# One Strassen level for the output projection of a gated mixer: w_out after wo, on row-scaled float16 y

## The chip, the cores and the metric

The kernel runs on one core of a Trainium2 chip. Its engines are TensorE (PE; its weight loads are listed as PEld), VectorE (DVE), ScalarE (ACT), GpSimd (POOL) and SyncE (SP), which issues all the transfers here. Each engine works through its own queue in program order; engines meet at semaphores. The metric is the device time of one execution in microseconds (us); of each kernel several executions were timed, and one more was profiled.

## The reference

With x of 2048 x 1024, the kernel computes

```python
g = sigmoid((x * gate_w).sum(-1, keepdims=True))
# a: 32 heads of 32; query s looks at keys s, s-2, ..., s-14
a = sliding_attention(x @ wqkv) @ wo            # wo: 1024 x 1024
z = gelu(x @ w_in)                              # w_in: 1024 x 3584
z1, z2 = z[:, :1792], layernorm(z[:, 1792:])
y = z1 * (w_sp @ z2 + b_sp[:, None])            # w_sp: 2048 x 2048
out = g * a + (1 - g) * (y @ w_out)             # w_out: 1792 x 1024
```

## The kernel before

All large buffers are slices of one SBUF tile, `arena`, so the profile names nearly every operand "arena"; line numbers tell them apart. A product is a run of matmuls over 128-row slices of the inner dimension that accumulate in one PSUM bank (`ps`, eight banks); an engine then copies the bank out.

TensorE's work comes in this order: two z2 column blocks of the first two row tiles and three more tiles of the first block (L577 to L579); heads of group 0 (`qkv_tile`, L535) and of groups 1 to 7, with the rest of z2's first block after group 1 (L580); the other z2 columns (L605); z1 (L624 to L642); the w_sp product (`g_group`, L669, called for n = 0 to 15; matmuls on L650); the w_out product (L728 to L736, matmuls on L734, 14 per bank, 32 banks); the wo product (L746 to L757, matmuls on L751, 8 per bank, 32 banks). VectorE computes attention, in steps of up to 4.4 us, from the first heads until far into the w_sp product, and DVE work of the other stages is put between those steps.

The order on the engines is written by a planner, `Beat` (L207). It counts TensorE's columns (`run`) as its clock. `at(t, fn)` puts `fn` on a heap, and at the end of each product (`run`, then `flush`) all that has come due is issued at that place of the program. Attention steps are issued by the planner when its count of VectorE's backlog falls under 3 us. So a due time fixes a place in each engine's queue, not a time: whatever stands there waits for its inputs, and all behind it on that engine waits too.

The w_sp product is already one Strassen level. Group n handles rows 256u to 256u+255 (u = n // 2) and half `fb` = n % 2 of the columns, with seven products of eight 448-column matmuls on float16 operands. Their sums t1 to t4 of z2 (`t_sums`, L463, and L643; the operation is on L461) and s1 to s4 of w_sp rows (`s_sums`, L454) are made on VectorE. In Python's words:

```python
product(pa, v.a11, b11, fb, True)     # P1
p1 = keep(pa, lo)                     # ScalarE copies the bank
product(pb, v.a12, b21, fb, True)     # P2
vec(g[:, 0, 0], pb[:, 0:ZC], p1)      # VectorE
product(pa, v.s2, t2, fb, False)      # P3 accumulates on P1's bank
u2 = keep(pa, lo)
product(pd, v.s1, t1, fb, True)       # P4
p5 = keep(pd, None)
product(pa, v.s3, t3, fb, False)      # P5
```

P6 accumulates in `pd` on P4, and P7 in `pa` on P5; after P7 ScalarE writes the last quarter (L689), and VectorE multiplies the whole by z1 (L690, `z` is the ring slot that held z1). `store_y` writes y to DRAM, from where it comes back transposed (`load_yT`, L507) as the stationary side of the w_out product. w_sp rows are scaled by a power of two per row (`row_norm`, L421; `row_power`, L424), so that float16 holds them; `omr` undoes it in the copy of w_out's banks (L735), and L740 adds the wo product times g.

SP's queue holds in order what the planner issues: w_sp rows by transposing DMA (`load_rows`, L443), z1 (`load_z1`, L492), y stores, transposed y, transposed attention outputs (`load_oT`, L415), w_out in two column halves (`load_w_out`, L510), wo (`load_wo`, L412).

## Time and profile before

| | us |
|---|---|
| median of 3 runs (698.88 to 702.46) | 699.11 |
| profiled execution | 699.66 |
| its span, first to last instruction | 697.9 |
| TensorE busy | 687.8 |
| VectorE busy | 467.8 |
| ScalarE busy | 293.5 |
| w_sp product, from its first matmul to w_out's | 370.4 to 542.4 |
| last attention step on VectorE | 484.6 |
| end of the last matmul | 694.1 |

A profile line such as "532.67 1.09 DVE L690 TENSOR_TENSOR arena<-arena 128x1792 bf16<-128x1792 bf16 x1 [1.55 <-ACT arena L689]" gives start and length in us, engine, line of the kernel, operation, output and inputs with their shapes, how many instructions were merged, and in brackets how long the engine stood idle before and what released it. SPq lines are the issuing of transfers, not the transfers. Rows of groups give busy time and the mean of one in ns. The chain of work that ended last is followed backwards from the last instruction through what released each step.

### The profile page before, as it was taken

Reading aid. Unit: us, or ns where it says so; the run is one execution under the profiler, and the core shown is the slowest. Engines: PE = TensorE matmul, PEld = TensorE weight load, DVE = VectorE, ACT = ScalarE, POOL = GpSimd, SP = SyncE. Lnnn points to the kernel's source line nnn. Section 1 sums busy time; section 2 is a strip of 40 time slices with the busy share of each in tenths; the row PEclk is TensorE's granted clock in tenths of the full one; section 3 lists DMA queues with packets and bytes.
Section 4 is the critical chain, followed back from the end, with each engine's and each line's share of the span. In section 5 each row is a group of like instructions: output and inputs, shape, how many; then the busy total and the mean of one; then the engine's idle time right before and its main releaser. Section 6 shows DMA issues by size and latency. Waiting matters only on the chain.

```text
span 697.9 us, 9291 instructions
## 1 busy us (share of the span) xinstructions
PE 687.8 (99%) x3667; PEld 401.0 (57%) x3681; DVE 467.8 (67%) x446; ACT 293.5 (42%) x562; POOL 13.7 (2%) x23
## 2 busy tenths in 40 slices
PE   8999999999999999999998999999999999999998
PEld 4577788888875555555554555555555444444443
DVE  0009899999999999999999999797552100001443
ACT  4255756565546968758332232322232222221000
POOL 1000000000000001021100000000000000000000
PEclk9999999999999999999999999999999999999999
DMA  8999649989869464534437655767999999000222
GB/s 238 180 244 259 189 105 269 258 240 235 220 169 246 173 212 139 165 113 165 149 103 212 115 146 144 200 166 174 179 213 256 214 199 234 1 0 16 75 76 76
DMA packets 234188, 118.13 MB, mean 169 GB/s; under 512 B 191009, under 2 KB 223521, under 8 KB 234145
## 3 DMA queue, kind: packets, MB, share of 16 engines
q1 hardware_dynamic: 234144, 117.54, 64.8%
q8 instruction: 29, 0.48, 0.3%
q14 instruction: 15, 0.11, 0.1%
HBM read 58.20 MB, written 37.82 MB: 138 GB/s over the span
## 4 chain that ended last, share of the span: by engine, by line
PE 95%; SPq 2%; DMA 1%; issue 1%; ACT 0%; DVE 0%; DVEq 0%
PE ps L535 24%; PE ps L650 23%; PE ps L634 14%; PE psb L734 14%; PE ps L281 12%; PE psa L751 8%; SPq L520 1%; DMA arena<-in_A_wqkv_dram 1%; DMA arena<-z_d 1%; SPq L518 0%; DVE arena L461 0%; SPq L249 0%; ACT L322 0%; SPq L516 0%; ACT arena L689 0%
## 5 line engine op out<-in xcount | busy, mean ns | idle before, releaser
L650 PE MATMUL ps<-arena 128*128 128x448 f16 x896 | 170.0, 353 | 2.2 <-DVE arena L461 2.0
L535 PE MATMUL ps<-arena 128*128 128x384 bf16 x1024 | 168.2, 328 | 2.4 <-DMA arena<-in_A_wqkv_dram 2.4
L535 PEld LDWEIGHTS <-arena 128*128 128x128 bf16 x1024 | 142.2, 139 | 28.5 <-issue 4.3
L650 PEld LDWEIGHTS <-arena 128*128 128x128 f16 x896 | 87.5, 98 | 84.6 <-DVE arena L461 2.5
L740 DVE SCALAR_TENSOR_TENSOR arena<-psa,g_s,arena 128x512 bf16<-128x512 f32 (+2 forms) x33 | 24.2, 735 | 126.5 <-PE psa L751 125.6
L304 DVE TENSOR_TENSOR arena<-arena 128x8192 bf16<-128x8192 bf16 x16 | 70.8, 4423 | 45.2 <-DMA arena<-k_d 44.9
L281 PE MATMUL ps<-arena 128*128 128x448 bf16 (+1 forms) x512 | 97.5, 353 | 0.1
L634 PE MATMUL ps<-arena 128*128 128x448 bf16 x512 | 97.2, 353 | 0.0
L734 PE MATMUL psb<-arena 128*128 128x512 bf16 x439 | 96.4, 379 | 0.5
L307 DVE TENSOR_TENSOR arena<-arena 128x4096 bf16<-128x4096 bf16 (+1 forms) x64 | 77.5, 1211 | 1.8
L634 PEld LDWEIGHTS <-arena 128*128 128x128 bf16 x512 | 49.9, 98 | 46.7
L281 PEld LDWEIGHTS <-arena 128*128 128x128 bf16 x512 | 49.9, 98 | 46.7 <-ACT arena L268 0.2
L734 PEld LDWEIGHTS <-arena 128*128 128x128 bf16 x448 | 43.8, 98 | 52.9
L543 ACT CAST arena<-ps 128x384 bf16<-128x384 f32 x112 | 51.1, 483 | 54.3 <-PE ps L535 51.8
L337 DVE TENSOR_TENSOR arena<-arena,att_A 128x8192 bf16<-128x8192 bf16 x16 | 70.8, 4422 | 0.7 <-DMA arena<-v_d 0.4
L662 ACT ACTIVATE arena<-ps,bt 128x448 f32<-128x448 f32 x48 | 30.4, 633 | 68.4 <-PE ps L650 68.4
L751 PE MATMUL psa<-arena 128*128 128x512 bf16 (+2 forms) x259 | 55.2, 373 | 0.3
L735 ACT ACTIVATE arena<-psb,omr 128x512 f32<-128x512 f32 x32 | 22.0, 687 | 74.8 <-PE psb L734 72.4
L636 ACT ACTIVATE arena<-ps 128x448 bf16<-128x448 f32 x64 | 33.5, 546 | 41.4 <-PE ps L634 34.7
L287 ACT ACTIVATE arena<-ps 128x448 bf16<-128x448 f32 x64 | 34.6, 549 | 25.3 <-PE ps L281 24.9
L751 PEld LDWEIGHTS <-arena 128*128 128x128 bf16 x264 | 25.5, 98 | 30.1
L343 DVE TENSOR_TENSOR arena<-arena 128x4096 bf16<-128x4096 bf16 x16 | 36.6, 2288 | 0.3
(77 smaller groups left out, 365.4 us busy)
## 6 DMA issues: line engine op xcount, KB each, us to landing
arena<-in_B_w_sp_dram SPq DMA_DIRECT2D x16, 512.0 KB, 4.4
arena<-k_d SPq DMA_DIRECT2D x8, 960.0 KB, 7.1
arena<-v_d SPq DMA_DIRECT2D x8, 960.0 KB, 5.2
z_d<-arena SPq DMA_DIRECT2D x16, 448.0 KB, 4.8
arena<-z_d SPq DMA_DIRECT2D x16, 448.0 KB, 3.7
y_d<-arena SPq DMA_DIRECT2D x32, 224.0 KB, 2.9
arena<-in_A_wqkv_dram SPq DMA_DIRECT2D x24, 256.0 KB, 6.6
arena<-in_B_w_in_dram SPq DMA_DIRECT2D x6, 896.0 KB, 6.6
```

The source lines that it names most:

```text
L281: nc.tensor.matmul(ps[:, 0:N], xT[:, kt, i * P:(i + 1) * P], w2[:, kt, ZC * c:ZC * c + N], start=(kt == 0), stop=(kt == KT - 1))
L287: nc.scalar.activation(z2[:, i, ZC * c:ZC * (c + 1)], ps[:, 0:ZC], ACT.Gelu_apprx_tanh, accum_out=s1[:, 4 * i + c:4 * i + c + 1])
L304: TT(prod.rearrange("p (w j c) -> p w j c", w=W, j=8, c=C), in0, in1, ALU.mult)
L307: return lambda: TT(pv[:, :, 0:half], pv[:, :, 0:half], pv[:, :, half:2 * half], ALU.add)
L337: TT(prod.rearrange("p (w j d h) -> p w j d h", w=W, j=8, d=DH, h=HG), in0, in1, ALU.mult)
L343: return [(4.4, mul), (2.3, lambda: TT(p3[:, 0:4, :], p3[:, 0:4, :], p3[:, 4:8, :], ALU.add)), (1.2, lambda: TT(p3[:, 0:2, :], p3[:, 0:2, ...
L535: nc.tensor.matmul(ps[:, 0:3 * C].rearrange("p (t c) -> p t c", t=3), lhsT, wgt[:, 0:3, kt, :], start=(kt == 0), stop=(kt == KT - 1))
L543: nc.scalar.copy(st[:, j % 4, :], ps[:, 0:3 * C])
L634: nc.tensor.matmul(ps[:, 0:ZC], xT[:, kt, i * P:(i + 1) * P], w1[:, kt, :], start=(kt == 0), stop=(kt == KT - 1))
L650: nc.tensor.matmul(ps[:, 0:ZC], w[:, k, :], v[:, k, fb * ZC:(fb + 1) * ZC], start=(first and k == 0), stop=(k == 7), skip_group_check=True)
L734: nc.tensor.matmul(psb[:], yT[a % 11][:, f, :], w_out_sb[c][:, f, :], start=(f == 0), stop=(f == NF - 1))
L751: nc.tensor.matmul(psa[:, 0:c1 - c0], oT[a][:, kt, :], wo_sb[:, kt, c0:c1], start=(kt == 0), stop=(kt == KT - 1))
```

## The change

- The wo product comes directly after the w_sp groups. Its banks are copied by ScalarE into `mix`, times g. wo and the transposed attention outputs are loaded as soon as attention has ended, beside the w_sp groups.
- The w_out product comes last and is one Strassen level: for each 256 rows, seven products of seven 512-column matmuls, on float16.
- For float16, y is scaled by a power of two per row. After each group, ScalarE sums |y| (`y_norm`, two instructions); after each second group VectorE makes the powers (`y_power`), ScalarE scales y in place (`y_scale`, four instructions), and SP stores it and loads the z1 of two pairs later (`y_done`). The multiply's ring of z1 slots is filled four ahead at the start.
- Beside the wo product, w_out is loaded in two halves, VectorE finds its largest magnitude (`w_peak`), a matmul with ones spreads it over the partitions (`w_power`), ScalarE and VectorE scale it in place (`w_scale`), and VectorE makes the sums (`w_sums`, `y_sums`).
- Six z2 tiles instead of three stand ahead of the first heads.
- t4 is made with the other sums, which come due 62 instead of 71 us after the start of the z1 stage; the last w1 block moves to another place in the arena and is loaded later.
- Buffers move: rows of y, w_out, its sums, wo and the output slots take over areas of the earlier stages.

```diff
--- before.py
+++ after.py
...
-    y_d = dpool.tile([S, FH], BF, name="y_d")
+    y_d = dpool.tile([S, FH], F16, name="y_d")
...
-                for o in (T4_OFF, T4_OFF + 3584, T2_OFF, T4_OFF)]
+                for o in (T4_OFF, T4_OFF + 3584, T2_OFF, SN_OFF)]
...
+    w_out_n = reg(X_OFF, NF * D)
+    w_out_h = reg(X_OFF, NF * D).bitcast(F16)
+    wv = w_out_h.rearrange("p (h k n) -> p h k n", h=2, n=D)
+    d11, d12, d21, d22 = [wv[:, h, :, 512 * c:512 * (c + 1)] for h in range(2) for c in range(2)]
+    e1, e2, e4 = [reg(F_OFF + 3584 * r, 3584).bitcast(F16).rearrange("p (k n) -> p k n", n=512) for r in range(3)]
+    e3 = d12
...
+    class Rows:
+        def __init__(self, off):
+            y = [reg(off + 1792 * r, 1792).bitcast(F16).rearrange("p (k t) -> p k t", t=P) for r in range(2)]
+            self.whole = y
+            self.a11, self.a12, self.a21, self.a22 = [y[r][:, 7 * h:7 * h + 7] for r in range(2) for h in range(2)]
+            self.s1, self.s2, self.s3 = [reg(off + 3584 + 896 * r, 896).bitcast(F16).rearrange(
+                "p (k t) -> p k t", t=P) for r in range(3)]
+            self.s4 = self.a21
...
+          for o in [A_OFF + 1024 * r for r in range(11)] + [S0_OFF + 1024 * r for r in range(5)]]
+    wo_sb = reg(A_OFF + 11264, KT * D).rearrange("p (k n) -> p k n", k=KT)
...
-        beat.at(t + 1.0, lambda: store_o(NG - 1))
+        beat.at(t + 1.0, attended)
+
+    def attended():
+        store_o(NG - 1)
+        load_wo()
         prep["attended"] = True
-        beat.at(max(t, prep["mixed"]) + 2.0, load_all_oT)
-
-    def load_all_oT():
-        for n in range(16):
-            beat.at(beat.now + 3.5 * n, lambda n=n: load_oT(n))
-
-    prep = {"at": 1e12, "normed": 0, "done": False, "mixed": 0.0, "attended": False, "y": 0}
...
-    def load_oT(n):
-        sync.dma_start_transpose(oT[n], o_d[n * P:(n + 1) * P, :])
+    def load_oT(limit):
+        n = prep["o"]
+        if n < limit:
+            sync.dma_start_transpose(oT[n], o_d[n * P:(n + 1) * P, :])
+            prep["o"] += 1
...
     def t_sums():
-        return [column_sum(o, a, b, fb) for o, a, b in ((t1, b12, b11), (t3, b22, b12), (t2, b22, t1))
+        return [column_sum(o, a, b, fb) for o, a, b in ((t1, b12, b11), (t3, b22, b12), (t2, b22, t1), (t4, b21, t2))
                 for fb in range(2)]
...
+    def load_rows_y(u):
+        for r in range(2):
+            sync.dma_start_transpose(rows[u % 5].whole[r], y_d[(2 * u + r) * P:(2 * u + r + 1) * P, :])
+
+    def y_norm(n):
+        for r in range(2):
+            k = 2 * (2 * (n // 2) + r) + n % 2
+            nc.scalar.activation(g_slots[n % 2][:, r], z1_ring[n % 4][:, r], ACT.Abs, accum_out=yl[:, k:k + 1])
+
+    def y_power(u):
+        sl = slice(2 * u, 2 * u + 2)
+        pair = yl[:, 4 * u:4 * u + 4].rearrange("p (r b) -> p r b", b=2)
+        TT(ys[:, sl], pair[:, :, 0], pair[:, :, 1], ALU.add)
+        nc.vector.tensor_scalar(ys[:, sl], ys[:, sl], 2.0 ** -30, 2.0 ** -11, ALU.max, ALU.mult)
+        nc.vector.tensor_scalar(ys[:, sl].bitcast(U32), ys[:, sl].bitcast(U32), EXPO, EXPO,
+                                ALU.bitwise_and, ALU.bitwise_xor)
+        beat.on_vector(0.3)
+
+    def y_scale(u):
+        for n in (2 * u, 2 * u + 1):
+            for r in range(2):
+                nc.scalar.activation(y_ring[n % 4][:, r], z1_ring[n % 4][:, r], ACT.Copy,
+                                     scale=ys[:, 2 * u + r:2 * u + r + 1])
+
+    def y_done(u):
+        store_y(2 * u)
+        store_y(2 * u + 1)
+        if u + 2 < NU:
+            load_z1(2 * u + 4)
+            load_z1(2 * u + 5)
...
-    for i in range(2, 5):
+    for i in range(2, 8):
         z2_tile(i, 0)
...
-            for i in range(5, 16):
+            for i in range(8, 16):
                 z2_tile(i, 0)
...
     t = beat.now
-    prep["at"] = t + 71.0
-    prep["mixed"] = t + (16 * 4 * KT + 2 * NU * 56) * ZC * BEAT
+    prep["at"] = t + 62.0
...
             load_w1(2)
-        if c == 1:
-            load_w1(3)
         for i in range(16):
+            if c == 2 and i == 6:
+                load_w1(3)
...
-    for fb in range(2):
-        column_sum(t4, b21, t2, fb)()
-        beat.on_vector(2.0)
...
+    def product(ps, w, v, c0, c1, first):
+        K = v.shape[1]
+        for k in range(K):
+            nc.tensor.matmul(ps[:, 0:c1 - c0], w[:, k, :], v[:, k, c0:c1], start=(first and k == 0),
+                             stop=(k == K - 1), skip_group_check=True)
+        beat.run(K * (c1 - c0))
...
         TT(z, g, z, ALU.mult)
         beat.on_vector(1.1)

-    for n in range(3):
+    for n in range(4):
         load_z1(n)
     for n in range(2 * NU):
         u, fb = n // 2, n % 2
         t = beat.now
...
+        if fb == 0 and u + 1 < NU:
+            beat.at(t + 0.5, lambda u=u: load_scale(u + 1))
+            for h in range(2):
+                beat.at(t + 0.5, lambda u=u, h=h: load_rows(u + 1, h))
         g_group(n)
-        if n + 3 < 2 * NU:
-            load_z1(n + 3)
-        beat.at(beat.now + 2.0, lambda n=n: store_y(n))
+        y_norm(n)
+        if fb == 1:
+            beat.at(beat.now + 2.0, lambda u=u: y_power(u))
+            beat.at(beat.now + 6.0, lambda u=u: y_scale(u))
+            beat.at(beat.now + 9.0, lambda u=u: y_done(u))
+        elif u + 1 < NU:
+            for h in range(2):
+                scale_rows(u + 1, h)
+            beat.on_vector(2.5)
+            for fn in s_sums(u + 1):
+                fn()
+            beat.on_vector(2.8)
         if prep["attended"]:
-            for m in range(2):
-                beat.at(beat.now + 3.0, lambda u=u: load_yT(min(2 * u, 11)))
-        if u + 1 < NU:
-            if fb == 0:
-                for h in range(2):
-                    scale_rows(u + 1, h)
-                beat.on_vector(2.5)
-                for fn in s_sums(u + 1):
-                    fn()
-                beat.on_vector(2.8)
+            limit = 16 if n >= 2 * NU - 3 else 11
+            for m in range(6):
+                beat.at(beat.now + 1.0 + 1.6 * m, lambda limit=limit: load_oT(limit))
+    assert prep["attended"]
...
     t = beat.now
-    assert prep["attended"]
-    beat.at(t + 0.5, lambda: load_w_out(1))
-    for m in range(11):
-        beat.at(t + 2.6, lambda: load_yT(11))
-    beat.at(t + 40.0, load_wo)
...
-    work = [(a, 0) for a in range(4)] + [(a, 1) for a in range(4)] + [(a, c) for a in range(4, 16) for c in range(2)]
-    for a, c in work:
-        if 0 < a < 6 and c == 1:
-            beat.at(beat.now + 0.5, lambda: load_yT(16))
-        psb = psum.tile([P, 512], F32, name="psb", tag="ps")
-        for f in range(NF):
-            nc.tensor.matmul(psb[:], yT[a % 11][:, f, :], w_out_sb[c][:, f, :], start=(f == 0), stop=(f == NF - 1))
-        nc.scalar.activation(mix[a][:, 512 * c:512 * (c + 1)], psb[:], ACT.Copy, scale=omr[:, a:a + 1])
-        beat.run(NF * 512)
-    beat.flush(1e9)
...
+    for m in range(16):
+        beat.at(t + 1.0 + 1.6 * m, lambda: load_oT(16))
+
+    def load_w_out(h):
+        sync.dma_start(w_out_n[:, 7168 * h:7168 * (h + 1)].rearrange("p (k n) -> p k n", n=D),
+                       B_w_out.rearrange("(h k p) n -> h p k n", h=2, p=P)[h])
...
+    ones = zeros[:].rearrange("p g c -> p (g c)")
...
+    def w_peak(h):
+        w = [w_out_n[:, 7168 * h + 896 * m:7168 * h + 896 * (m + 1)] for m in range(8)]
+        top, low = abs_waste[:, 0:896], abs_waste[:, 896:1792]
+        for out_, op in ((top, ALU.max), (low, ALU.min)):
+            TT(out_, w[0], w[1], op)
+            for m in range(2, 8):
+                TT(out_, out_, w[m], op)
+        nc.vector.scalar_tensor_tensor(top, low, -1.0, top, ALU.mult, ALU.max)
+        nc.vector.tensor_reduce(wl[:, h:h + 1], top, AX.X, ALU.max)
+
+    def w_power():
+        TT(wl_n[:], wl[:, 0:1], wl[:, 1:2], ALU.max)
+        ps = psum.tile([P, 512], F32, name="ps", tag="ps")
+        nc.tensor.matmul(ps[:, 0:1], ones, wl_n[:], start=True, stop=True)
+        nc.vector.tensor_scalar(wsc[:], ps[:, 0:1], 2.0 ** -30, 2.0 ** -11, ALU.max, ALU.mult)
+        nc.vector.tensor_scalar(wsc[:].bitcast(U32), wsc[:].bitcast(U32), EXPO, EXPO, ALU.bitwise_and, ALU.bitwise_xor)
+
+    def w_scale(m):
+        sl = slice(2048 * m, 2048 * (m + 1))
+        if m < 3:
+            nc.scalar.activation(w_out_h[:, sl], w_out_n[:, sl], ACT.Copy, scale=wsc[:])
+        else:
+            nc.vector.tensor_scalar(w_out_h[:, sl], w_out_n[:, sl], wsc[:], None, ALU.mult)
+
+    def omegas():
+        for x in (ys[:], wsc[:]):
+            nc.vector.tensor_scalar(x.bitcast(U32), x.bitcast(U32), EXPO, EXPO, ALU.bitwise_and, ALU.bitwise_xor)
+        nc.vector.scalar_tensor_tensor(omr[:], ys[:], 0.5, omr[:], ALU.mult, ALU.mult)
+        nc.vector.tensor_scalar(omr[:], omr[:], wsc[:], 0.5, ALU.mult, ALU.mult)
+
+    def w_sums():
+        for out_, a, b in ((e1, d12, d11), (e2, d22, e1), (e3, d22, d12), (e4, d21, e2)):
+            TT(out_, a, b, ALU.subtract)
+
+    def y_sums(u):
+        v = rows[u % 5]
+        TT(v.s1, v.a21, v.a22, ALU.add)
+        TT(v.s3, v.a11, v.a21, ALU.subtract)
+        TT(v.s2, v.s1, v.a11, ALU.subtract)
+        TT(v.s4, v.a12, v.s2, ALU.subtract)
+
+    beat.at(t + 0.5, lambda: load_w_out(0))
+    beat.at(t + 9.5, lambda: load_w_out(1))
+    beat.at(t + 1.0, lambda: nc.vector.memset(zeros[:], 1.0))
+    beat.at(t + 11.0, lambda: w_peak(0))
+    beat.at(t + 19.0, lambda: w_peak(1))
+    beat.at(t + 31.0, w_power)
+    for m in range(7):
+        beat.at(t + 31.5 + 2.0 * (m % 3), lambda m=m: w_scale(m))
+    beat.at(t + 37.0, w_sums)
+    beat.at(t + 39.0, omegas)
+    for u in range(2):
+        beat.at(t + 26.0 + 4.0 * u, lambda u=u: load_rows_y(u))
+        beat.at(t + 44.0 + 4.0 * u, lambda u=u: y_sums(u))

     for a in range(16):
-        cuts = [0, 512, D] if a < 15 else [0, 512, 896, D]
-        for c0, c1 in zip(cuts, cuts[1:]):
+        if a == 12:
+            beat.at(beat.now + 0.5, lambda: load_rows_y(2))
+        for c in range(2):
             psa = psum.tile([P, 512], F32, name="psa", tag="ps")
             for kt in range(KT):
-                nc.tensor.matmul(psa[:, 0:c1 - c0], oT[a][:, kt, :], wo_sb[:, kt, c0:c1],
+                nc.tensor.matmul(psa[:], oT[a][:, kt, :], wo_sb[:, kt, 512 * c:512 * (c + 1)],
                                  start=(kt == 0), stop=(kt == KT - 1))
-            combine(psa, a, c0, c1)
-            if a == 15:
-                store(a, c0, c1)
-        if a < 15:
-            store(a, 0, D)
+            nc.scalar.activation(mix[a][:, 512 * c:512 * (c + 1)], psa[:], ACT.Copy, scale=g_s[:, a:a + 1])
+            beat.run(KT * 512)
+    beat.flush(1e9)
...
+    def hold(ps, scale):
+        out = keeps[kept[0] % 7]
+        kept[0] += 1
+        nc.scalar.activation(out, ps[:], ACT.Copy, scale=scale)
+        return out
...
+    def finish(out, ps, scale, x):
+        nc.vector.scalar_tensor_tensor(out, ps[:], scale, x, ALU.mult, ALU.add)
+
+    for u in range(NU):
+        v = rows[u % 5]
+        lo, hi = [omr[:, 2 * u + h:2 * u + h + 1] for h in range(2)]
...
+        pa, pb, pd = [psum.tile([P, 512], F32, name="ps", tag="ps") for _ in range(3)]
+        if u == 0:
+            for n in (3, 4):
+                load_rows_y(n)
+        product(pa, v.a11, d11, 0, 512, True)
+        p1 = hold(pa, lo)
+        product(pb, v.a12, d21, 0, 512, True)
+        TT(p1, p1, m11, ALU.add)
+        finish(o11, pb, lo, p1)
+        product(pa, v.s2, e2, 0, 512, False)
+        u2 = hold(pa, lo)
+        product(pd, v.s1, e1, 0, 512, True)
+        p5 = hold(pd, hi)
+        TT(u2, u2, m12, ALU.add)
+        product(pa, v.s3, e3, 0, 512, False)
+        u3 = hold(pa, hi)
+        TT(p5, p5, m22, ALU.add)
+        if 0 < u < NU - 1:
+            y_sums(u + 1)
+        product(pd, v.s4, d22, 0, 512, False)
+        TT(o22, p5, u3, ALU.add)
+        finish(o12, pd, lo, u2)
+        sync.dma_start(out2[2 * u * P:(2 * u + 1) * P, :], ob_slots[2 * u])
+        product(pa, v.a22, e4, 0, 512, False)
+        finish(o21, pa, hi, m21)
+        if u == NU - 1:
+            sync.dma_start(out2[(2 * u + 1) * P:(2 * u + 2) * P, 512:D], o22)
+            sync.dma_start(out2[(2 * u + 1) * P:(2 * u + 2) * P, 0:512], o21)
+        else:
+            sync.dma_start(out2[(2 * u + 1) * P:(2 * u + 2) * P, :], ob_slots[2 * u + 1])
+        if u + 5 < NU:
+            load_rows_y(u + 5)

...
```

77 lines of the change are left out of this document (32 added, 45 removed).

## The prediction

> **What bounds the kernel now.** I read the page's busy shares first, then its chain, then the timeline of single groups.
>
> ```profile
> PE 687.8 (99%) x3667; PEld 401.0 (57%) x3681; DVE 467.8 (67%) x446; ACT 293.5 (42%) x562; POOL 13.7 (2%) x23
> PE   8999999999999999999998999999999999999998
> DVE  0009899999999999999999999797552100001443
> PE 95%; SPq 2%; DMA 1%; issue 1%; ACT 0%; DVE 0%; DVEq 0%
> PE ps L535 24%; PE ps L650 23%; PE ps L634 14%; PE psb L734 14%; PE ps L281 12%; PE psa L751 8%; SPq L520 1%; DMA arena<-in_A_wqkv_dram 1%; DMA arena<-z_d 1%; SPq L518 0%; DVE arena L461 0%; SPq L249 0%; ACT L322 0%; SPq L516 0%; ACT arena L689 0%
> ```
>
> TensorE never rests, so fewer matmuls are worth their full time, and every wait put into its stream costs its full time too. The change works in three stages: the w_sp groups (L650, 370.4 to 542.4 us; DVE is nearly full until 484.6, when attention ends), w_out (L734, to 639.9), wo (L751, to 694.1). The next lines are one group of the first stage without attention beside it, and one in which ScalarE was late.
>
> ```profile
> 532.00 0.63 ACT L689 ACTIVATE arena<-ps,bt 128x448 bf16<-128x448 f32 x1 [2.34 <-PE ps L650]
> 532.67 1.09 DVE L690 TENSOR_TENSOR arena<-arena 128x1792 bf16<-128x1792 bf16 x1 [1.55 <-ACT arena L689]
> 533.58 0.63 ACT L662 ACTIVATE arena<-ps,bt 128x448 f32<-128x448 f32 x1 [0.94 <-PE ps L650]
> 536.61 0.63 ACT L662 ACTIVATE arena<-ps,bt 128x448 f32<-128x448 f32 x1 [2.39 <-PE ps L650]
> 538.06 0.53 ACT L660 COPY arena<-ps 128x448 f32<-128x448 f32 x1 [0.82 <-PE ps L650]
> 539.62 0.63 ACT L662 ACTIVATE arena<-ps,bt 128x448 f32<-128x448 f32 x1 [1.03 <-PE ps L650]
> 542.60 0.63 ACT L689 ACTIVATE arena<-ps,bt 128x448 bf16<-128x448 f32 x1 [2.35 <-PE ps L650]
> ...
> 404.57 0.63 ACT L689 ACTIVATE arena<-ps,bt 128x448 bf16<-128x448 f32 x1 [2.35 <-PE ps L650]
> 405.22 1.28 ACT L322 ACT_TABLE_LOAD   x1
> 406.51 0.63 ACT L322 ACTIVATE att_L<-att_L 128x512 f32<-128x512 f32 x1
> 407.05 0.61 ACT L662 ACTIVATE arena<-ps,bt 128x448 f32<-128x448 f32 x1
> 407.71 3.57 PE L650 MATMUL ps<-arena 128*128 128x448 f16 x18 [0.16 <-ACT arena L662]
> ```
>
> A group lasts 10.60 us (L689 to L689), so each of its seven products P1 to P7 takes 1.513. P1, P3, P5, P7 accumulate in one bank `pa`, and ScalarE copies it out after each (P1's copy at +1.58). P3 may not start before P1's copy has ended, and it would start at 3.03. At 404.57 a table load and an exp stood in front of that copy; it ended at 407.66, 3.09 after the group's end, and TensorE restarted at 407.71. The trace thus shows the slack (about 0.1 us above 3.0) and that a later copy stalls TensorE one for one.
>
> **The change part by part.** The sum is made against the profiled execution, 699.66 us with a span of 697.9 and 1.8 around it; the median of the three runs, 699.11, lies 0.55 lower.
>
> *w_out product.* 448 matmuls become 8 x 7 x 7 = 392. 49 take 10.79 on the chain (from 553.62 to 564.41), or, if the merged row leaves its first out, 50, so 0.216 each (97.5 us for 448 is 0.218): -56 x 0.216 = **-12.1**. float16 streams no slower: L650 and L634 both show 353 ns at 448 columns. Inside the new stage a round of seven products lasts 10.6; ScalarE has 4 x 0.69 in it, DVE 4 f32 sums (L319: 0.69), 3 finishes (L740: 0.75) and 4 sums for the next round (L457: 0.69 for 1024, so about 0.62 for 896), 7.5 in all. The order of copies is that of the w_sp groups, which run without a stall when both engines are quick: 0.
>
> *y_norm.* Two Abs of 896 elements per group go into ScalarE's queue behind L689 and ahead of the next group's copies, and read the product of L690. By the 1708 ns of L599 at 1792 and the 1920 of L422 at 2048 (0.83 ns per element), 0.97 each; the accumulator reads overlap (59.80, then 61.61 and 61.70: a pitch of 1.90). From a group's end at 0: L689 to 0.66, L690 to 1.76, Abs to 3.73, P1's copy to 4.37, P3 at 4.42 instead of 3.03. Stall 1.4, in 15 groups (the first has none before it): **+21.0**. Behind the last group the wo products follow, whose banks are eight: 0.
>
> *y_scale.* Four Copies of 896 with a scale, due 6.0 after an odd group's end, in the next group. Four products make 6.07 on the plan's clock, so they land in ScalarE's queue behind P3's copy and ahead of P4's (p5). P6 accumulates on P4's bank and waits for p5. With the stall above, P3 ends at 5.93, its copy at 6.61, four Copies (0.97 each, 0.09 more for the scale, by L662's 633 against L660's 532) at 10.5, p5 at 11.05, P6 starts at 11.1 instead of 8.96: 2.1, in seven groups (the eighth falls beside wo): **+14.7**. y_power, which they wait for, is three DVE operations of 0.17 behind the Abs, done by 4.4.
>
> *DVE's lateness.* L690 was harmless when late; now ScalarE's queue stands behind it. In groups 0 to 9 it started 4.3, 3.1, 4.0, 1.7, 1.2, 0.0, 3.2, 0.3, 1.0, 0.6 after L689's end, 19.4 in all (384.06 to 388.39 the first). Bounds 0, because stalls of TensorE let DVE catch up, and 19.4. The first groups inherit a backlog, and a 4.42 us attention step can still stand directly ahead of L690; I take about half, **+9**. SP's queue has a new wait too: y_done's stores wait for y_scale and the z1 loads behind them for the stores (four issues of 0.6, 2.9 landing), so SP serves nobody else for about 5 in every second group. z1 is needed two groups later, which covers it; attention's k and v loads behind may be late, and that lies in the upper half of this term. The exps (0.63) in the same queue and a y_power behind an attention step: 0 to 8, **+3**.
>
> *The clock.* These rows are stretches of 3.4 us with PE busy in the second column, the granted clock third from the end.
>
> ```profile
> 14.90:18.30 3.40, 1.34 (x8) 0.58 (x6) 0.00 (x0) 1.13 (x4) 0.00 (x0) 1.00 1.06 222
> 18.30:21.70 3.40, 3.04 (x10) 1.43 (x10) 0.00 (x0) 0.28 (x2) 0.00 (x0) 0.51 1.40 160
> ...
> 380.10:383.50 3.40, 1.85 (x10) 0.99 (x11) 3.40 (x3) 0.07 (x1) 0.00 (x0) 1.00 1.00 244
> 383.50:386.90 3.40, 3.40 (x20) 1.76 (x18) 3.40 (x5) 1.20 (x2) 0.00 (x0) 1.00 0.15 57
> ```
>
> A stretch with 1.34 busy was followed by one at half clock, which costs half of 3.4, 1.7; one with 1.85 busy was not. A 2.1 us stall, or a 1.4 one lengthened by DVE, leaves 1.3 of 3.4 where it falls inside one stretch, about every second time: some 3.5 of 17 such stalls at 1.7, **+6**, bounds 0 and 20 (twelve). The Trainium skill ("TensorE: Matmul & The Clock Gate", HAM oscillation) lets the clock drop only for gaps over about 3.4 us; a gap of 2.42 did it here, so row and rule differ, and by the rule this term would be 0 and the sum 6 lower (rival e).
>
> *z1 stage.* t4 moves ahead of the groups (L461, two of 2.0), and w1's last slot moves out of its way. TensorE waited 2.04 for it in group 0: **-2.0** (0 if DVE is late still: this work was due at 273.3 + 71 = 344 and began at 353).
>
> *Early z2 tiles.* Three tiles (1.51 each) go ahead of the first heads. TensorE idled 2.42 there, to 18.66, for weights. But tiles 6 and 7 need transposes issued behind those weights (from 15.64, 1.47 each, 4.5 to landing): tile 5 ends at 17.75, tile 6 starts near 20, and the heads follow at about 23.5 instead of 18.66 + 4.5. Between -2.4 and +2, **+0.5**. Attention begins some 4 later, inside DVE's lateness above.
>
> *w_power beside wo.* It is a matmul in TensorE's queue behind the 18th of 32 wo products (18 x 1.73 = 31.1 after the groups), and waits for DVE's maxima over all of w_out. On SP, the first half starts when the last group has read `pairs[1]` (9.4 to landing by w_out's row; I take 7.5 to 9.4 with less traffic beside it), at about 9. The second waits for the y stores: y_scale behind four evictions, 7.6 to 11.6; four store issues of 0.6 and 2.9 landing, 17; landed at 25 to 26. A half's maxima are 14 operations of 0.62 and two of about 1.0, 10.7 us, so the second ends near 36.5, and TensorE stands 5.5; a half-clock stretch follows, 1.7: **+7**. Bounds 0 and +13 (maxima at the 0.98 that f32 tensor operations of that size would take by L319). Everything behind (w_scale to 43, w_sums 4 x 2.02 to 51, y_sums to 56) ends before wo does, near 61. Scaling on ScalarE (three of 1.9) hides behind eight banks. The two rows_y loads (four transposes, 4.7 to landing) start at 26, long before 53. Loads of wo and oT now run beside the groups, after attention: the DMA of y's transposes leaves that place, so it is hidden.
>
> *Tail.* Last matmul, a 0.75 finish, a 128 KB store (1.7 to landing): as before, 0 +/- 0.5.
>
> Sum: 699.66 - 12.1 + 21.0 + 14.7 + 9 + 3 + 6 - 2.0 + 0.5 + 7 = **746.8**, about 747.
>
> **Rivals.** (a) *ScalarE's new work hides.* The place is P1's copy: it must end within 3.0 of a group's end. That needs the Abs pair done at 2.4 instead of 3.73, so 0.6 us for two of 896, and y_scale under 1.8 instead of 3.9. Then 699.66 - 12.1 - 2.0 + 0.5, with 0 to 7 at w_power: 686 to 693, faster. The 42% of ScalarE speak for it, the chain at 404.57 against it. 8%. (b) *Bare stalls.* DVE catches up at once and the clock holds: without 9, 3 and 6, with 0 to 7 at w_power, 722 to 729. The pace of DVE after 484.6 (L690 0.04 behind L689) speaks for it, the full DVE before against it. 18%. (c) *Lateness and clock together.* DVE stays as late as it was (+10), and the lengthened stalls halve the clock nine times instead of 3.5 (+9): 766, and 772 with the upper bound of w_power. For it speaks that DVE is in order behind attention, against it that stalls are time for DVE. 18%. (d) *Rewriting gains nothing*, because the new stage waits for its sums: 7.5 of DVE in 10.6 speaks against it; the stage would last 97 instead of 84.6 and the time be 759, inside the forecast's range: 2%. (e) *The clock holds* through all gaps under 3.4 us, with DVE's lateness as summed: 741. The row at 380.10 speaks for it, the one at 14.90 against it. 10%.
>
> **How the numbers follow.** Forecast 747 (735 to 760), 42%. The range leaves out (a) and the outermost of (b) and (c): 720 to 776. About 0.5% (3.5 us) is what a measurement of this kernel can tell from none. Faster 8%, from (a); the same 2%, between (a) and (b); slower 90%, all others.
>
> **What would show it.** On ScalarE, in each group: the pair of Abs behind the multiply, and only then P1's copy. On TensorE: an idle of 1.4 or more ahead of P3 in every group and of about 2 ahead of P6 in every second, released by ScalarE; a group stage of 172 + 52; one idle of about 5 at the single-column matmul beside wo; a new w_out stage of 84.6. It is wrong if the groups keep 10.6, if ScalarE runs the Abs in another place, or if the multiply comes much later than DVE's lags before.

## The result, and the profile after

The changed kernel takes 749.73 us (median of 4 runs, 745.80 to 750.97), the kernel before 700.15 beside it (698.88 to 702.46): the ratio is 1.0695, with a 95% interval of 1.0641 to 1.0748. It is 7% slower. The profiled execution took 750.97 us, its span is 749.2, the mean granted clock 0.977.

The page's busy shares, its slices and its chain by engine, of the kernel after (the chain can be followed back only to 492.82 us, so its shares of the span are small):

```profile
PE 689.0 (92%) x3612; PEld 397.4 (53%) x3618; DVE 538.7 (72%) x573; ACT 379.0 (51%) x693; POOL 13.1 (2%) x23
PE   8999999999999999999958887867789798999998
PEclk9999999999999999999988998998999999999999
PE 22%; ACT 6%; DVE 3%; DMA 2%; issue 1%; SPq 0%; ACTq 0%; DVEq 0%
```

TensorE has holes now, from slice 21 to slice 32, and its clock dips in four of them: that is the w_sp stage. The groups of matmuls by their shapes, and the waits (released by, total us, times, longest):

```profile
L695 PE MATMUL ps<-arena 128*128 128x448 f16 x896 | 182.5, 365 | 50.3 <-ACT arena L707 37.4 <-ACT arena L705 12.9
L695 PE MATMUL ps<-arena 128*128 128x512 f16 x392 | 84.8, 379 | 0.0
...
PE ps L695 <- ACT arena L707: 37.4, 15, 10.0
PE ps L695 <- ACT arena L705: 12.9, 7, 1.8
ACT arena L538 <- DVE arena L736: 35.7, 16, 9.8
PE ps L790 <- DVE wl_n L788: 2.0, 1, 2.0
```

L707 and L705 are ScalarE's copies of a bank (`keep`), L538 is `y_norm`'s Abs, L736 the multiply, L790 `w_power`'s matmul. TensorE waits 15 times ahead of P3 and 7 times ahead of P6 for ScalarE, as the prediction placed it, and ScalarE waits 16 times for the multiply. The w_out stage runs without any wait. One such place on the chain of work, with start and length:

```profile
539.03 0.64 ACT arena L735
539.70 1.10 DVE arena L736
540.83 1.98 ACT arena L538 x4
542.80 0.53 ACT arena L707
543.37 7.74 PE ps L695 x40
```

Last quarter, multiply, two Abs with their accumulator reads, P1's copy, P3: each waits for the one ahead, and none runs beside another. By stages, the profiled executions compare like this (us):

| stage | before | after | difference | forecast |
|---|---|---|---|---|
| start to first w_sp matmul | 370.4 | 370.7 | +0.3 | +0.5 |
| w_sp groups | 172.0 | 232.8 | +60.8 | +51.7 |
| wo | 54.9 | 57.4 | +2.5 | +7 |
| w_out | 96.8 | 84.6 | -12.2 | -12.1 |
| tail | 3.8 | 3.6 | -0.2 | 0 |

The 60.8 of the w_sp groups are 50.3 of waits instead of 2.2, and 896 matmuls of 448 columns that are busy for 182.5 instead of 170.0, most of it by half clock (the run with fillers, below, parts the two).

### The profile page after: what moved, and what is told of

It reads as the page before. It is cut to its first block, busy times and chain, and to the rows that moved or that the text cites. A ratio compares the mean times of both kernels' runs of the same rounds, so it can differ in the third digit from the quotient of the medians.

```text
span 749.2 us, 9446 instructions
## 1 busy us (share of the span) xinstructions
PE 689.0 (92%) x3612; PEld 397.4 (53%) x3618; DVE 538.7 (72%) x573; ACT 379.0 (51%) x693; POOL 13.1 (2%) x23
## 5 line engine op out<-in xcount | busy, mean ns | idle before, releaser
L695 PE MATMUL ps<-arena 128*128 128x448 f16 (+1 forms) x1288 | 267.3, 369 | 50.3 <-ACT arena L707 37.4
L695 PEld LDWEIGHTS <-arena 128*128 128x128 f16 x1288 | 128.3, 100 | 188.9 <-issue 67.5
L584 PEld LDWEIGHTS <-arena 128*128 128x128 bf16 x1024 | 141.7, 138 | 25.0 <-issue 0.2
L306 PE MATMUL ps<-arena 128*128 128x448 bf16 (+1 forms) x512 | 99.6, 357 | 2.5 <-DMA arena<-in_A_x_dram 2.4
L306 PEld LDWEIGHTS <-arena 128*128 128x128 bf16 x512 | 50.3, 99 | 50.6 <-DMA arena<-in_A_x_dram 3.0
L682 PEld LDWEIGHTS <-arena 128*128 128x128 bf16 x512 | 50.0, 98 | 46.6
L362 DVE TENSOR_TENSOR arena<-arena,att_A 128x8192 bf16<-128x8192 bf16 x16 | 70.7, 4420 | 0.2
L838 PE MATMUL psa<-arena 128*128 128x512 bf16 x250 | 55.3, 379 | 0.3
L684 ACT ACTIVATE arena<-ps 128x448 bf16<-128x448 f32 x64 | 33.4, 553 | 41.6 <-PE ps L682 32.1
L849 ACT ACTIVATE arena<-ps,omr 128x512 f32<-128x512 f32 x32 | 22.0, 688 | 59.6 <-PE ps L695 59.6
L707 ACT ACTIVATE arena<-ps,bt 128x448 f32<-128x448 f32 x48 | 30.1, 627 | 43.3 <-PE ps L695 43.3
L538 ACT ACTIVATE arena<-arena 128x896 bf16<-128x896 bf16 x32 | 30.1, 942 | 35.7 <-DVE arena L736 35.7
L711 DVE TENSOR_TENSOR arena<-arena 128x448 bf16<-128x448 f32 x16 | 10.0, 624 | 51.2 <-ACT arena L707 51.2
L838 PEld LDWEIGHTS <-arena 128*128 128x128 bf16 x256 | 25.0, 98 | 29.9
L368 DVE TENSOR_TENSOR arena<-arena 128x4096 bf16<-128x4096 bf16 x16 | 36.6, 2288 | 0.3
L840 ACT ACTIVATE arena<-psa,g_s 128x512 f32<-128x512 f32 x32 | 21.5, 685 | 24.0 <-PE psa L838 24.0
```

The lines of the kernel that those rows point to most:

```text
L306: nc.tensor.matmul(ps[:, 0:N], xT[:, kt, i * P:(i + 1) * P], w2[:, kt, ZC * c:ZC * c + N], start=(kt == 0), stop=(kt == KT - 1))
L362: TT(prod.rearrange("p (w j d h) -> p w j d h", w=W, j=8, d=DH, h=HG), in0, in1, ALU.mult)
L368: return [(4.4, mul), (2.3, lambda: TT(p3[:, 0:4, :], p3[:, 0:4, :], p3[:, 4:8, :], ALU.add)), (1.2, lambda: TT(p3[:, 0:2, :], p3[:, 0:2, ...
L538: nc.scalar.activation(g_slots[n % 2][:, r], z1_ring[n % 4][:, r], ACT.Abs, accum_out=yl[:, k:k + 1])
L584: nc.tensor.matmul(ps[:, 0:3 * C].rearrange("p (t c) -> p t c", t=3), lhsT, wgt[:, 0:3, kt, :], start=(kt == 0), stop=(kt == KT - 1))
L682: nc.tensor.matmul(ps[:, 0:ZC], xT[:, kt, i * P:(i + 1) * P], w1[:, kt, :], start=(kt == 0), stop=(kt == KT - 1))
```

## The experiments

The theory: ScalarE's queue is in order, so the cost comes from where the new work stands ahead of copies that TensorE needs, above all where it waits there for a late multiply. The rivals: the work itself costs (its time on ScalarE, or what it slows elsewhere), or the clock is a loss of its own.

### Other places for the same work (three kernels)

`y_norm` behind P1's copy of the next group instead of ahead of it:

```diff
-        y_norm(n)
+        beat.at(beat.now + 2.0, lambda n=n: y_norm(n))
```

> The changed kernel with one thing moved: the two Abs of a group (y_norm) are put into ScalarE's queue behind the next group's copy of P1 instead of ahead of it. Same instructions, same amount of work. Queue theory (the loss is the place of the new instructions ahead of copies that TensorE waits for): the bare wait ahead of P3, 15 x 1.37 = 20.5 us, goes; of the 16.9 us that DVE's late multiplies added there, what exceeds about 1.2 per late group stays, some 12; y_scale keeps its 13 to 15; part of the 12.5 of half clock goes. 749.7 - 20.5 - 5 - 4 = 720 us. Work theory (ScalarE simply has 7 us of work more in two groups, wherever it stands): 745 to 750. Elsewhere theory (the new order of products and loads costs the time): 745 to 750.

Measured: 716.34 us (715.94 to 716.57), ratio 1.0232 (1.0215 to 1.0250). Moving two instructions behind one copy gave back 33 of the 50 us that the change costs. The waits:

```profile
PE ps L695 <- ACT arena L705: 14.3, 7, 2.7
PE ps L695 <- ACT arena L707: 8.8, 3, 6.9
```

The 15 waits ahead of P3 are gone. Three are left, 6.9, 0.9 and 1.0 us, and they stand ahead of P5, which needs P3's copy: that copy is now the first behind the Abs pair. The 7 ahead of P6 stayed. Next, `y_scale` alone, its four Copies one or two at a time behind three different copies:

```diff
-            beat.at(beat.now + 6.0, lambda u=u: y_scale(u))
-            beat.at(beat.now + 9.0, lambda u=u: y_done(u))
+            for part, due in enumerate((6.07, 7.59, 9.11, 9.11)):
+                beat.at(beat.now + due, lambda u=u, part=part: y_scale(u, part))
+            beat.at(beat.now + 10.6, lambda u=u: y_done(u))
```

In this kernel and the next, `y_done` of the last pair comes so late that the second half of w_out is loaded over that pair's y before it is stored. So part of the output is not what the reference gives, and that load beside wo waits for less than it should; the groups are not touched by it.

> The changed kernel with one thing moved: the four Copies of y_scale no longer stand in a row ahead of P4's copy; one stands behind P3's copy, one behind P4's, two behind P5's, and the stores of y are issued 1.6 us later. Queue theory: the seven waits ahead of P6 (12.9 us in all) go and the waits ahead of P3 stay: 749.7 - 12.9 = 737 us. Work theory and elsewhere theory: 747 to 750.

Measured: 734.38 us (733.12 to 735.18), ratio 1.0494 (1.0472 to 1.0517). The waits ahead of P6 are gone, those ahead of P3 are as they were. Then both edits together:

> The two moves of the runs before together. Queue theory: 20.5 and 12.9 go, of DVE's lateness some 12 of 17 stays, of the half clock less than half: 749.7 - 33.4 - 5 - 7 = 704 us, 698 to 712. If lateness of DVE's multiply is what really stalls and the rest only follows it: above 715. Work theory: 745 to 750.

Measured: 707.05 us (706.02 to 707.98), ratio 1.0100 (1.0079 to 1.0120). The first row is of the `y_scale` edit alone, the second of both:

```profile
PE ps L694 <- ACT arena L706: 38.0, 15, 10.0
...
PE ps L694 <- ACT arena L706: 15.5, 5, 7.1
```

The three came within 4 us of the queue theory's 720, 737 and 704, where the work theory had 745 or more for each. The gains are 33.4 and 15.4 us alone and 42.7 together. No work was taken away, so its place is worth some 43 of the 50 us (at most 2.0 of it, `w_power`'s wait, can be the load that doesn't wait). The 15.5 us that remain stand in five places, all ahead of P5, each behind a late multiply.

### The work left out, and the early z2 tiles

Here the scaling of y is left out (`y_norm`, `y_power`, `y_scale`): the multiply writes float16 y into the ring, and `ys` is set to 1.

```diff
-        TT(z, g, z, ALU.mult)
+        TT(y_ring[n % 4], g, z, ALU.mult)
...
-        y_norm(n)
```

> The changed kernel without the row scaling of y: no Abs sums, no powers, no in-place scaling; VectorE's multiply writes y as float16 directly. All else, the order of wo and w_out, the loads, w_out's scaling and the Strassen rounds, is kept. Queue and work theory alike: the group stage returns to about 170 us, so 749.7 - 50.3 (waits) - 12.5 (half clock) = 687 us, 684 to 692, and faster than before by what the 56 matmuls are worth. Elsewhere theory: still above 730. DVE theory (DVE is too full for the stage whatever ScalarE does): above 700.

Measured: 688.24 us (686.70 to 689.58), ratio 0.9831 (0.9807 to 0.9854). The gain of the w_out product, that of t4 and a shorter wait for `w_power` (0.8) are all there. So the whole loss came with the scaling of y. The same with three early z2 tiles, as before the change:

```diff
-    for i in range(2, 8):
+    for i in range(2, 5):
...
-            for i in range(8, 16):
+            for i in range(5, 16):
```

> The kernel without y's row scaling (688.2), with three z2 tiles ahead of the first heads as before, not six. My price for the six was +0.5 us (between -2.4 and +2), since the early idle of TensorE is only moved from the heads' weights to the transposes of tile 6; so 687.7, 686 to 690.5. If the six tiles do cover the early wait: 690 to 691.

Measured: 685.11 us (684.67 to 685.18), ratio 0.9778 (0.9759 to 0.9798). The six tiles cost 3.1 us, not the half microsecond that this expectation and the prediction gave them. Of the w_sp groups' matmuls:

```profile
L696 PE MATMUL ps<-arena 128*128 128x448 f16 x896 | 169.8, 352 | 0.2 <-ACT arena L708 0.2
```

Waits in the groups fell from 1.8 to 0.2, with attention beginning earlier. The idle ahead of the heads was 1.93, for their weights, instead of 2.57, for x's transposes, and no half clock came behind it. How much of the second is the tiles' doing stays open, as in the kernel before 2.42 us of idle did halve the clock there. But it is not all of the 3.1: the two runs with six tiles that show a granted clock of 1.000 took 686.70 and 687.71 us.

The same edit on the changed kernel itself, with its scaling:

> The changed kernel with one part undone: three z2 tiles ahead of the first heads, as before, so that attention starts on VectorE some 4.5 us earlier. Without y's scaling this was worth 3.1 us. If it is worth only that (early idle and the half clock behind it): 749.7 - 3.1 = 746.6, 745 to 748, and the waits ahead of P3 stay at 37. If VectorE's late multiplies (16.9 of those waits) come from attention's later start: the late waits fall by some 4 in group 1 and go in groups 5, 8 and 9, the half clock with them: 749.7 - 3 - 12 - 8 = 727, 722 to 735.

Measured: 741.36 us (738.44 to 742.57), ratio 1.0594 (1.0560 to 1.0623): 8.4 us gained, between the two expectations. The waits ahead of P3 fell from 37.4 to 32.4, and the matmuls' busy time from 182.5 to 177.4. Attention's later start is one cause of the late multiplies; some 12 us of lateness stay without it.

### Is the clock a loss of its own?

More matmuls of 448 columns, into a spare bank and ahead of P3, keep TensorE busy where it would wait; none of the results uses them.

```diff
+        count = {0: 0, 1: 48, 2: 9, 5: 20, 8: 19, 9: 20}.get(n, 6)
...
+                nc.tensor.matmul(pf[:, 0:ZC], v.a11[:, k % 8, :], b11[:, k % 8, f0:f1], start=True, stop=True)
         product(pa, v.s2, t2, f0, f1, False)
```

> The changed kernel, and in the time that TensorE stands ahead of P3 it repeats matmuls into a spare bank that nobody reads: 48 (9.1 us) in group 1, 9 in group 2, 19 or 20 in groups 5, 8 and 9, 6 (1.1 us) in the others, each a little less than the wait seen there. No engine gets less to do and no wait is taken away. Clock theory (the half-clock stretches, which cost 12.5 us of matmul time in the group stage, come from TensorE standing still, and add to the waits): the clock holds and the time falls to about 738, 735 to 742. If the half clock falls where VectorE is late anyway, so that TensorE, being faster, only waits for VectorE longer: the clock holds and the time stays above 744. If the clock falls for another reason: half-clock stretches remain and 749 to 751.

Measured: 742.82 us (739.79 to 744.34), ratio 1.0599 (1.0560 to 1.0639): 6.9 less than the changed kernel, between the two expectations.

```profile
L695 PE MATMUL ps<-arena 128*128 128x448 f16 x896 | 173.3, 352 | 17.1 <-ACT arena L705 12.9 <-ACT arena L707 4.2
```

The groups ran at full clock, and their stage was 9.1 shorter (223.6): the matmuls gained 9.2 (182.5 to 173.3). Less these and the 12.9 ahead of P6, 37.4 of the stage are left for fillers and waits ahead of P3, as much as the waits alone had taken. So the half clock was a real loss of some 9 us, on top of the waits. The 173.3 also show that of the 12.5 more than before, 3.3 are not the clock: 0.15 at each of the 22 places where the stream still breaks (a matmul's record is 352 ns long, and the next one starts after 189, a group's 10.60 us over 56).

### Is it the Abs, or what it waits for?

The Abs pair in the same place, reading a buffer that is ready; its sums are not those of y.

```diff
-            nc.scalar.activation(g_slots[n % 2][:, r], z1_ring[n % 4][:, r], ACT.Abs, accum_out=yl[:, k:k + 1])
+            nc.scalar.activation(reg(SN_OFF + 2688, 896), reg(Z_OFF, 896), ACT.Abs, accum_out=yl[:, k:k + 1])
```

> The changed kernel, with the two Abs of each group at the same place in ScalarE's queue and of the same size, but over data that has long been there, written to a spare place (the ring of copies has five slots instead of six for it). The powers of y are then taken from other data; the scaling itself is kept. Queue theory: the Abs now end at 0.66 + 1.9 = 2.6 after a group's end and P1's copy at 3.2, so the wait ahead of P3 is 0.2 instead of 1.37 and does not know of VectorE's lateness: 37.4 falls to 3 to 5; the half clock goes; y_scale keeps its 13: 749.7 - 33 - 11 = 705 us. If the Abs themselves are the cost (their 1.9 us, not the wait for the multiply in front of them): the wait stays near 20 and the time above 725.

Measured: 712.47 us (710.29 to 713.22), ratio 1.0165 (1.0139 to 1.0191).

```profile
PE ps L695 <- ACT arena L705: 17.0, 8, 3.9
PE ps L695 <- ACT arena L707: 3.4, 15, 0.3
```

Of the 37.4 us ahead of P3, 34.0 were the wait for the multiply. The pair's own 1.9 us are worth 0.22 in each group: they fill the gap between two groups, while ScalarE waits for P1 anyway. The time stayed 7.5 above the expectation; 4.1 of it are the waits ahead of P6, which grew to 17.0, and 3.7 are matmul time: it fell by 7.3, to 175.2, and not by the 11 that I had put down to the clock.

### Later and later places

All of the change, with the Abs one by one behind P3's and P4's copies of the next group, `y_power` behind its P6, and the four Copies two behind P5's copy and two behind P1's a group later:

```diff
+            beat.at(e + 6.07, lambda n=n: y_norm(n, (0,)))
+            beat.at(e + 7.59, lambda n=n: y_norm(n, (1,)))
...
+            power, dues, done = (9.11, (9.11, 9.11, 13.66, 13.66), 14.0)
```

> All of the change, scaling included, in another order on ScalarE: each group's two Abs stand one behind P3's copy and one behind P4's copy of the next group, where the multiply may be 3.4 us late at no cost; the four Copies of y_scale stand two behind P5's copy of that group and two behind P1's copy one group later; the stores follow; the ones-matmul stands one wo product later. Queue theory: no bare waits, of VectorE's lateness only group 0's beyond 3.4, some 3 to 5; no half clock but the early one: 749.7 - 33.4 - 12 - 11 - 2 = 691 us, 688 to 696, faster than before. Work theory: over 700, since ScalarE's 7 us more in two groups are all still there.

Measured: 697.16 us (696.33 to 698.42), ratio 0.9957 (0.9939 to 0.9974). It does all that the change does, and is not slower than before. It missed its expectation by one to six us; these rows of TensorE's timeline begin behind the three waits that are left:

```profile
391.35 25.12 PE L694 MATMUL ps<-arena 128*128 128x448 f16 x120 [4.57 <-ACT arena L704]
417.46 15.29 PE L694 MATMUL ps<-arena 128*128 128x448 f16 x80 [0.99 <-ACT arena L706]
436.02 115.34 PE L694 MATMUL ps<-arena 128*128 128x448 f16 x600 [3.27 <-ACT arena L706]
```

After 436 us nothing waits. The same with three early z2 tiles:

> All of the change with y's scaling, in the order of the run that puts the copies first (697.2), and three z2 tiles ahead of the first heads. If the six tiles cost the 3.1 us that they cost without the scaling: 694. If VectorE's lateness comes from them: its 8.8 us of waits and the 5 of half clock behind them go too, 686 to 690. Faster than before either way.

Measured: 697.40 us (694.54 to 700.52), ratio 0.9971 (0.9954 to 0.9987). No gain: 9.3 us of waits (one of 4.51) against 8.8, so both expectations missed. The multiply of group 1, behind which the longest wait stands, begins 20.2 us after the first group's start in both traces: with attention earlier, two more of its steps (2.28 and 1.22) stand ahead of that multiply.

So the Abs pair went behind P5's copy, and the Copies into the group after that:

```diff
+            beat.at(e + 9.11, lambda n=n: y_norm(n))
...
+            power, dues, done = (10.62, (13.66, 13.66, 16.70, 18.21), 18.3)
```

> All of the change, with ScalarE's added instructions moved later in the plan, and three z2 tiles ahead of the first heads as before: the Abs pair behind P5's copy of the next group (so that a late multiply has some 6 us more before ScalarE's queue reaches it), the scale Copies one group later still, behind copies of P1, P3 and P4, and the first store of a pair of y tiles earlier. The two versions with the Abs pair split behind the copies of P3 and P4 measured 697.2 us (six z2 tiles) and 697.4 us (three); the latter's TensorE waits in the group stage were 9.3 us, 4.51 of them at group 1, with two half-clock stretches behind them. By the theory of queue order and late multiplies those waits go (at most 2.5 us stay, for the exponentials' own), and with them the half clock: 697.4 - 6.5 - 3.5 = 687 us (685 to 692). If the added work of ScalarE and VectorE itself costs the rest (ports, pace of the copies), it stays at 695 us or above; the same would be seen if the later stores of y made SyncE's queue late, with the waits then at the exponentials' or at w_power.

Measured: 696.24 us (695.22 to 697.02), ratio 0.9959 (0.9942 to 0.9976): by the queue theory 687 was due, so it missed. ScalarE's timeline and VectorE's show where the wait went (L551 the Copies, L545 `y_power`, L362 and L368 attention):

```profile
409.45 1.98 ACT L551 ACTIVATE arena<-arena,ys 128x896 f16<-128x896 bf16 x2 [5.13 <-DVE ys L545]
...
401.25 4.42 DVE L362 TENSOR_TENSOR arena<-arena,att_A 128x8192 bf16<-128x8192 bf16 x1
...
406.65 2.28 DVE L368 TENSOR_TENSOR arena<-arena 128x4096 bf16<-128x4096 bf16 x1
...
409.25 0.17 DVE L545 TENSOR_SCALAR ys<-ys 128x2 uint32<-128x2 uint32 x1
```

Of the waits of the Abs one of 0.86 us is left in the groups, and it does not reach TensorE. Now the first Copy waits 5.13 us for three tiny VectorE operations that stand behind attention steps. This happens twice (pairs 0 and 2), and TensorE loses 7.6 us there and 3.5 by half clock (173.3 against 169.8). That is all: 685.11 + 7.6 + 3.5 = 696.2, the time measured. Apart from these two places, the scaling of y costs nothing that shows.

The last kernel puts the first two Copies two and three products later and the other two four and five later, and it stores y and reloads z1 tile by tile (the last pair but one keeps its places):

```diff
+            power, dues, done = (10.62, (16.70, 18.21, 24.29, 24.29), 24.6)
```

> The version with the Abs pair behind P5's copy measured 696.24 us; its TensorE waits in the group stage are 7.8 us in 3, and they are no longer the Abs pair's: ScalarE stands 5.13 and 4.51 us before the first scale Copy of the pairs 0 and 2, because y_power is queued on VectorE behind attention steps of 4.4 us, the second of them itself waiting 2.61 us for v's load, which SyncE issues behind the stores of y. Here each pair's first two Copies come two products later (behind P3's and P4's copies of the second group after), the other two behind P1's copy of the group after that, and the store of y and the reload of z1 are issued tile by tile, so that SyncE is held for half as long at once. By the theory of queue order the two late ones shrink to what exceeds 3 us, 2.1 and 1.5 us, under the 1.3 us of slack or little over it: TensorE waits of 1 to 2 us, no half clock in the group stage (448-column matmuls 170 instead of 173.3 us): 696.2 - 6 - 3.4 = 687 us (685 to 690). If the added instructions themselves set the pace, or the loads of z1 come late for the multiply now, 694 us or more, with waits that name z1's load or VectorE.

Measured: 699.86 us (697.86 to 702.58), ratio 1.0010 (0.9995 to 1.0025): not 687, but no different from before. The waits of TensorE:

```profile
PE ps L694 <- ACT arena L704: 5.8, 2, 4.6
PE ps L800 <- DVE wl_n L798: 5.2, 1, 5.2
```

The wait at pair 0 fell from 4.44 to 1.16, as expected. The one at pair 2 did not, and its chain runs through SP's queue:

```profile
440.80 2.54 DMA y_d<-arena
443.40 0.38 SPq L521
...
443.83 6.06 DMA arena<-v_d
...
449.98 4.43 DVE arena L362
454.41 0.08 DVE ys L543
```

SP waits for the store of y before it reloads that slot with z1 (L521); attention's v is loaded behind that, the 4.43 us step behind v, and `y_power` behind the step. And `w_power` now waits 5.2 us instead of 0.6: TensorE came there 3.2 earlier and the maxima 1.4 later, as the first half of w_out took 9.5 us to land instead of 7.5, with y's stores ahead of it and beside it. The stage of the groups was 2.5 us shorter than in the kernel ahead (178.4 against 181.0), wo was 6.3 longer (62.1 against 55.8). The theory of ScalarE's queue had left out SP's.

## Why the prediction was right, point by point

The forecast of 747 was 3 us under the measured 749.73 (and 4.2 under the profiled 750.97), and the mechanism is the one that it named: ScalarE's new work ahead of the copies that TensorE waits for, late multiplies, and half clock behind the longer waits. Its terms:

- **w_out product**: -12.2 for -12.1, 392 matmuls in 84.6 us, no waits in it.
- **y_norm**: 15 waits of 1.35 to 1.37 where no lateness was added, 20.5 for 21.0.
- **y_scale**: 12.9 for 14.7. The four Copies took 3.83, 0.96 each, and each stall 1.84 instead of 2.1.
- **DVE's lateness** was undersized: 37.4 less 20.5 are 16.9, for 9 + 3. Over half of it, 8.7, is one group:

```profile
391.95 0.95 ACT L538 ACTIVATE arena<-arena 128x896 bf16<-128x896 bf16 x1 [9.79 <-DVE arena L736]
```

The multiply began at 390.83, behind a 4.43 us attention step that had begun at 385.24 and two sums of 0.62. Lateness did not come down with the stalls, since each new attention step can stand ahead of a multiply again: in the groups 5, 8 and 9 a step of 4.42 us (from 445.21, 487.87 and 506.68) stood ahead of it, directly or with one sum between, and the wait ahead of P3 was 3.91 to 4.04. It is the term of this sum that deserved its upper end.

- **The clock**: 9.2 for 6 by the run with fillers, and the way I counted it was wrong. These are stretches of 3.4 us (PE busy in the second column, granted clock third from the end), around a wait of 4.04 and, below the line of dots, one of 1.84:

```profile
448.10:451.50 3.40, 1.08 (x6) 0.46 (x5) 1.00 0.38 107
451.50:454.90 3.40, 1.69 (x5) 0.69 (x5) 0.50 0.49 110
454.90:458.30 3.40, 3.40 (x10) 1.32 (x9) 0.50 0.00 0
...
413.95:417.36 3.41, 1.57 (x9) 0.75 (x8) 1.00 0.60 207
417.36:420.77 3.41, 3.41 (x20) 1.77 (x19) 1.00 0.85 209
```

The stretches are fixed: in this trace half clock begins at 21.41, 386.64, 451.49, 495.87 and 512.93 us, all whole multiples of 3.413 apart. At full clock, a stretch with 1.08 busy is followed by half clock, one with 1.57 is not, though all of a 1.84 us wait lies in it. With the 1.34 of the kernel before, the limit lies between 1.34 and 1.57 of 3.4 (the trace of the later places with three tiles narrows it: 1.39 was followed by half clock, 1.43 was not). A stretch that itself runs at half clock needs more: the one with 1.69 was followed by another. So the bare stalls never tripped it, and I had let every second one do so; the late ones, of 3.9 to 10, tripped it each time, and a long wait also leaves the stretch after it short, so that two or more halve. All nine half-clock stretches of this stage lie at the four waits of 3.9 and more. That the term came within some 3 us is luck: the stretches were more than I took, and lay behind fewer stalls.

By the rule of the Trainium skill ("TensorE: Matmul & The Clock Gate", HAM oscillation) only a gap over some 3.4 us lowers the clock. Here the waits of 3.9 and more did, which agrees, but so did the idle times ahead of the heads, 2.42 us before and 2.37 after: what counts in these rows is the idle share of one stretch. The next section of that page of the Trainium skill (A second HAM failure mode) says that frequent short idles between matmul groups, from cycling through PSUM banks, can also make the clock swing; 15 idles of 1.35 and more and 7 of 1.84 in this stage did so only where a late multiply made them long.

- **t4**: its 2.0 are gone, as said.
- **Early z2 tiles**: the start of the groups moved by 0.3, for 0.5. But their price was larger and lies elsewhere too: 3.1 us without the scaling (in part open, as said there), 8.4 with it, where a later attention also makes multiplies late.
- **w_power**: 2.0 for 7, and no half clock behind it. The second half of w_out landed at 21.1 us after the groups instead of 25 to 26, so the maxima ended at 33.0 for 36.5. The 0.98 of its upper bound does not follow from L319 alone, whose 0.69 is for 512 columns; the maxima took 0.62 to 0.63 each.
- **A reading**: w_out in the kernel before ends at 639.2, not at 639.9; the first matmuls of wo stand between. The price of 0.216 a matmul, which the sum used, is not touched by it.

The errors cancel by half, +9.1 in the groups and -4.5 beside wo, so that the total is closer than its parts is luck too. Of the rivals, (a) is out: ScalarE does not hide this order of work. But the two sides stand closer together than I thought, since the same work a few products later in ScalarE's queue ran at 696.24. (b), bare stalls, fails at the 16.9 of lateness. (c) put lateness at +10 above mine and the half-clock stretches at nine: nine they were, but two of them, from 386.64 on, fell into a wait and cost nothing, and the lateness was only 4.9 above; its 766 is out. (d) is out, the w_out stage ran in 84.6. (e), full clock, did not happen, but what it priced at 6 is worth 6.9 by the run with fillers (9.2 in the groups, less 2.0 beside wo, where that run had a half-clock stretch and the changed kernel none).

Open: why VectorE is as late as it is in the first groups. Attention's later start is a part (the six tiles cost 8.4 us on the changed kernel, 3.1 without the scaling, nothing in the version with later places), and SP's queue is another (v's load, in the last kernel). No run separates the rest.

## What to carry to other kernels

When work is given to an engine that is 42% busy, its share says nothing of the cost: ask which copy the bottleneck waits for next, and what stands ahead of it in that in-order queue. Two Abs of 0.95 us cost 37 us ahead of P1's copy because they wait for a multiply, and nothing in the gap behind P5's copy, where the data are ready. Delay has its own bill, paid in the next queue: the fastest version with the scaling takes 696.24 us (0.4% faster than before), and one more delay sent the loss to SP's loads; leaving the scaling of y out, which changes what is computed in float16, gives 685.11 (2.2% faster).

## What the runs showed of the hardware that I had not expected

The clock goes by the busy time within fixed stretches of 3.4 us, so the same wait can cost or not by where it falls. `w_power`'s wait of 2.1 us in the kernel with `y_norm` behind P1's copy fell into one stretch, the 2.0 us of the changed kernel across two:

```profile
596.65:600.07 3.42, 1.29 (x8) 0.43 (x6) 3.04 (x5) 0.80 (x2) 0.00 (x0) 1.00 1.19 244
600.07:603.48 3.41, 3.19 (x8) 1.22 (x8) 3.05 (x6) 0.05 (x1) 0.00 (x0) 0.50 0.20 44
...
632.36:635.77 3.41, 2.22 (x11) 0.78 (x8) 3.27 (x5) 1.37 (x2) 0.00 (x0) 1.00 1.16 259
635.77:639.18 3.41, 2.54 (x12) 1.21 (x14) 3.03 (x8) 0.64 (x2) 0.00 (x0) 1.00 0.48 105
```

The first pair halved the clock for one stretch, the second did not.
